# A new order for a kernel of recurrent attention and a gated layer: transfers moved between queues, transposes moved between TensorE and DMA

## The chip, the cores and the metric

The kernel runs on one core of a Trainium2 chip. The time is device time in microseconds (us) of one execution, as a median over several. Engines are named as the profile names them: PE is TensorE (PEld its weight loads), DVE is VectorE, ACT is ScalarE, POOL is GpSimd, SP is SyncE; SPq, ACTq and POOLq are the transfers that these engines issue.

## The reference, cut to what matters

```
def _attn_ref(r, k, v, w, u):                  # B, H, S, D = 4, 8, 768, 48
    state = zeros((B, H, D, D))
    for t in range(S):
        cur = einsum('bhd,bhe->bhde', u[None] * k[:, :, t], v[:, :, t])
        y[:, :, t] = einsum('bhd,bhde->bhe', r[:, :, t], state + cur)
        state = w[:, :, t, :, None] * state + einsum('bhd,bhe->bhde', k[:, :, t], v[:, :, t])

def _moe_ref(x, w_in, w_out, g_ln):            # x is y as (3072, 384); w_in 384 x 1024, w_out 1024 x 384
    h = x @ w_in
    e = exp(h - max(h));  sm = e / (sum(e) + 1e-09)
    solu = h * sm
    ln = (solu - mean(solu)) / sqrt(var(solu) + 1e-06) * g_ln
    return ln @ w_out
```

All inputs and the output are float32.

## The kernel before

The 768 steps of each of the 4 batches are cut into 6 chunks of 128 tokens. A chunk of a batch is a *unit*; the 24 units are numbered so that unit i is chunk i // 4 of batch i % 4. Within a chunk the recurrence is written as matrix products (scores between tokens, with decays folded into k and r), and a state of 384 columns goes from one chunk of a batch to the next. Each unit then goes through the second layer: hidden product, exponential, product, square, output product, scaling.

There are no loops over units in the program text. `ORDER` is a string of words written in one sequence; a word is a stage, a unit number and, after a point, how it is done. A loop at the end of the kernel calls the stage for each word:

```
    for word in ORDER.split():
        word, _, how = word.partition(".")
        name = word.rstrip("0123456789")
        stages[name](int(word[len(name):]), how)
```

Every engine goes through its own part of this sequence in order (`InOrder` ties each instruction to the one before it on the same engine); between engines only data dependences and reuse of buffers hold. Buffers are rings: 7 tiles for each loaded input, 10 for `lw` and `vb`, 6 for `kp`, `kr` and `dv`, 4 for the others. PSUM has four single slots (`s0` to `s3`) and two double ones (`b0`, `b1`), named in the word. A transfer that SP or ACT issues also waits, in the built program, for the completion of the transfer eight places before it among those of SP and ACT together, since eight semaphores are used in turn; those of POOL have eight of their own.

The words of one unit, in the order of its data:

- `LW`, `LK`, `LR`, `LV` load w, k, r and v, 192 KB each in rows of 48 floats; the letter after the point is the issuing engine (`s` SP, `a` ACT, `p` POOL). `LI0` to `LI2` load w_in (512 KB each), `LO0` and `LO1` w_out (768 KB each), `LU` and `LG` u and the gain.
- `lw` is the logarithm of w (ACT), `cum` its cumulated sums (PE, two products), `ex` the exponentials of these (ACT), `kp` the scaled k and r (DVE). `p`, `q` (POOL) and `dg` (DVE), `dv` (POOL) make the term with u. `vb` rounds v to bf16.
- `krk` and `krr` transpose the scaled k and r on PE, four products each, and `kr` copies them out of PSUM (DVE or ACT). `KD` in their place is one DMA transpose issued by SP, from `kp` straight to `kr`.
- `M` is the scores (8 products), `m` their copy to SBUF: by DVE with the mask in one instruction, or by ACT with the mask as `sel` on POOL. `S`, `et`, `st` are the state.
- `Y` is the attention output. With `n` the term `dv` is added by DVE in `y`, with `i` PE adds it with one more product and ACT copies. `X` and `xT` transpose y (PE, then a copy by DVE or ACT), or `XD` does it by DMA.
- `H` is the hidden product, `e` its exponential (ACT), `he` the product of both (DVE), `hq` the squares (ACT), `Oa` and `Ob` the output product in two halves. `sq`, `qm`, `lv` give the scale, `o` applies it (DVE or ACT), `out` stores 192 KB (by SP unless a letter says otherwise).
- For units that have the word `HD`, the hidden product is turned the other way, tokens in the rows: six products with 512 columns instead of 24 with 128, sums from ACT's accumulator instead of from products with a column of ones, and `HD` transposes `he` by DMA before `Oa`.
- `hot` makes dummy products on a tile of zeros, as many as its number says, which nobody reads. `wi`, `gw`, `mn` and `ce` prepare the weights; the last unit's layer is cut into halves (`Ha`, `Hb`, ... `Mal`, `outl`, `outr`).

The lines that the steps below touch:

```
    by_token = {int(word[2:]) for word in ORDER.split() if word[:2] == "HD"}
    def turned_kr(i, x):
        sp.dma_start_transpose(out=kr_s[i % NKP], in_=kp_t[i % NKP].rearrange("t j h d -> t (j h d)"))
    def load_v(i, x):
        queue[x].dma_start(out=v_t[i % NIO], in_=rows_of(v, i))
```

Of the kernel before, what the change touches and what calls it, by code (L numbers as in the profile page):

```python
# [26 lines left out]
dg2 krk4.s0 LK5.s m3.d krr4 vb2.a p4 H0.b0 y1.a kr4.a dg3 dv2 st0 et1 e0 LR5.s M4.b1 LV4.p S2.s3 m4.d Y2.ns0
X1.s1 et2 gw0.a LW6.s q4 lw5 he0 gw1.a LK6.s cum5.b1 vb3.p gw2.a gw3.p st1 ex5 xT1.d S3.s2 st2 H1.b0 gw5.a dv3
y2.d gw6.a dg4 LR6.s gw7.p gw4.a Y3.is1 e1 X2.s3 LW7.s kp5 mn0.s0 vb4.p y3.a he1 p5 xT2.a LK7.s lw6 X3.s1 et3
krk5.s3 hq0 dv4 ce1 cum6.b1 LR7.s H2.b0 ce5 LV5.p ex6 ce3 LW8.s ce2 xT3.a p6 krr5 ce0 e2 Y4.is1 LK8.s kp6 LV6.p  # L30
y4.a he2 lw7 LR8.s S4.s1 kr5.a q5 H3.b1 LW9.s ce7 LV7.p hq1 ce4 M5.b0 LK9.s ce6 e3 q6 X4.s3 st3 Oa0.s0 m5.d
LR9.s vb5.p hq2 krk6.s2 p7 Ob0 lw8 he3 LW10.s xT4.a krr6 q7 cum7.b0 et4 sq0 vb6.a Oa1.s3 LK10.s qm0 kr6.d ex7
LV8.p dg5 cum8.b1 hq3 S5.s2 kp7 p8 LR10.s Ob1 ex8 st4 LV9.p LW11.s H4.b0 dg6 lw9 kp8 lv0 p9 LK11.s et5 o0.a
krk7.s1 dg7 sq1 e4 M6.b1 LV10.p st5 LR11.s krr7 Oa2.s0 qm1 kr7.d vb7.a q8 LW12.s m6.a he4 S6.s2 Ob2 dv5 et6 lv1
st6 LK12.s dv6 M7.b1 o1.a cum9.b0 m7.d sq2 lw10 Y5.ns1 q9 LR12.s ex9 Oa3.s3 p10 y5.d lw11 cum10.b1 qm2 kp9
LW13.s X5.s2 lv2 Ob3 sel6 ex10 xT5.d LK13.s dg8 cum11.b0 o2.a vb8.p krk8.s1 kp10 krk9.s2 ex11 p11 krr8 out0
Y6.ns0 sq3 kr8.d krr9 hq4 H5.b1 vb9.p LR13.s kp11 dv7 kr9.a qm3 dg9 q10 LW14.s krk10.s1 e5 M8.b0 y6.d Oa4.s2 dv8
m8.d LK14.s lw12 X6.s0 LR14.s LV11.p lv3 krr10 Ob4 he5 lw13 o3.a out1.p LW15.s M9.b0 xT6.a dg10 krk11.s3 p12
m9.a cum12.b1 kr10.d LK15.s Y7.ns0 krr11 q11 ex12 y7.d S7.s1 LR15.s kr11.d H6.b0 sq4 hq5 dv9 kp12 LV12.s q12 et7
lw14 X7.s0 st7 Y8.ns3 e6 p13 qm4 M10.b1 xT7.d y8.d S8.s1 out2 m10.a he6 krk12.s0 vb10.p S9.s3 sel9 LV13.s krr12  # L40
et8 et9 cum13.b1 lv4 st8 H7.b0 ex13 dg11 dv10 LW16.s st9 kr12.a vb11.p kp13 Oa5.s1 LK16.s out3.p e7 LR16.s o4.d
S10.s0 p14 krk13.s3 lw15 he7 M11.b1 LW17.s et10 out4.p krr13 m11.a X8.s2 Ob5 sel10 kr13.d LK17.s hq6 cum14.b0
st10 vb12.p M12.b1 dg12 LR17.s ex14 S11.s3 q13 m12.d Oa6.s0 sq5 xT8.a sel11 hq7 Y9.ns2 kp14 cum15.b1 q14 Ob6
et11 ex15 qm5 y9.d KD14 st11 p15 H8.b0 lv5 kp15 lw16 LW18.s o5.a vb13.p dg13 LK18.s X9.s2 LV14.p sq6 Y10.ns3 e8
xT9.d KD15 Y11.ns1 qm6 y10.d S12.s2 dv11 lw17 he8 cum16.b1 lv6 Oa7.s3 LR18.s LV15.p o6.a y11.d et12 LV16.s ex16
M13.b0 dv12 dg14 Ob7 st12 m13.a dv13 LW19.s kp16 X10.s0 Y12.ns1 xT10.a out5.p M14.b0 lw18 H9.b1 m14.d out6.p sq7
# [5 lines left out]
H13.b1 qm10 dg17 ex19 out8.p xT14.d o9.d dv16 lv10 kp19 Y15.ns1 e13 S15.s3 vb17.p S16.s2 o10.d out9.p KD19 hq11
H14.b0 y15.d sel16 he13 lw21 LV21.s et15 et16 vb18.p Oa11.s0 LK22.s e14 st15 q18 LR22.s cum20.b1 hq12 Y16.ns1
he14 vb19.p Ob11 q19 ex20 st16 M18.b0 p20 sq11 X15.s3 y16.d m18.a S17.s2 xT15.d Oa12.s1 vb20.p kp20 et17 hq13
sel17 cum21.b0 qm11 st17 KD20 H15.b1 lv11 dg18 q20 ex21 o11.d out10 dv17 Ob12 e15 kp21 LW23.s sel18 X16.s3
LK23.s S18.s2 lw22 he15 KD21 Oa13.s0 et18 out11.p hq14 LV22.p M19.b0 dg19 M20.b1 HD15 sq12 m19.a xT16.d Ob13
qm12 m20.d p21 lv12 Y17.ns3 lw23 cum22.b0 vb21.p y17.d H16.b1 ex22 dv18 st18 dg20 o12.a dv19 kp22 Y18.ns3 sq13
e16 out12 X17.s2 sel19 Oa14.s1 LR23.s qm13 y18.d hq15 KD22 xT17.d M21.b0 q21 he16 Y19.ns3 X18.s2 Ob14 m21.a dv20
xT18.d HD16 y19.d p22 cum23.b1 sq14 lv13 dg21 H17.b0 ex23 o13.d dv21 qm14 out13 kp23 X19.s2 sel21 Y20.ns3 e17
S19.s0 xT19.d KD23 H18.b1 y20.d q22 lv14 he17 hq16 p23 XD20 Oa15.s2 o14.d et19 e18 q23 M22.b0 st19 Ob15 HD17  # L60
vb22.p m22.a Oa16.s3 he18 Y21.ns1 LV23.s hq17 sel22 M23.b0 y21.d Ob16 m23.d XD21 sq15 hq18 H19.b1 qm15 dg22 HD18
sq16 lv15 qm16 Y22.ns0 dg23 dv22 e19 Oa17.s1 o15.d vb23.p H20.b0 y22.d lv16 dv23 he19 XD22 Ob17 e20 out14 H21.b1
HD19 sq17 hq19 he20 Y23.ns2 Oa18.s0 out15 e21 o16.d HD20 H22.b0 y23.d hq20 qm17 he21 out16 Ob18 e22 HD21 X23.s3
Oa19.s2 xT23.d lv17 he22 Ha23.b1 sq18 hq21 Ob19 qm18 HD22 Hb23 sq19 ea23 qm19 o17.d Oa20.s3 lv18 out17 lv19
o18.d Oa21.s1 eb23 o19.d Ob20 out18.p hq22 hea23 out19 Ob21 sq20 hqa23 Oa22.s0 qm20 heb23 sq21 lv20 Sa23.s2 qm21
hqb23 Ob22 o20.d lv21 Sb23 out20 sq22 Mal23.s3 qm22 sq23 o21.d lv22 Mbl23 qm23 out21 Mar23.s1 o22.d lv23 Mbr23
# [558 lines left out]
```

## Time and profile before

| | us |
|---|---|
| median of 3 timed runs | 148.57 |
| lowest, highest of them | 147.11, 152.67 |
| the profiled execution | 151.26 |
| its span, first to last instruction | 149.6 |

| engine | busy us | share of the span |
|---|---|---|
| PE | 130.8 | 87% |
| DVE | 122.4 | 82% |
| ACT | 122.5 | 82% |
| POOL | 112.3 | 75% |

The page gives the busy share of each engine in 40 slices of the span, with PEclk, the clock that TensorE was granted, in tenths; then the chain of work that ended last, followed back from the end; then groups of instructions and transfers. In the chain, a piece named DMA is time in which the next instruction waited for that transfer. The matmul durations of the groups overlap, so the cost of a product on PE is read from the chain, where starts follow each other: 1.34 us for the 24 hidden products of a unit, 1.66 for its output products (1.32 where `HD` is used), 0.33 for scores, 0.33 for cum, 0.46 for state, 0.37 for Y, 0.17 for X, 0.45 for the 8 transposes of k and r. Every instruction of the stages is recorded at one helper's line (L87), so groups are told apart by their tiles.

### The profile page before, as it was taken

What the parts mean: (1) busy time and instruction counts of PE and PEld (TensorE: products, weight loads), DVE (VectorE), ACT (ScalarE), POOL (GpSimd) and SP (SyncE); (2) the same over time, 40 slices, a digit from 0 to 9 for tenths busy, and PEclk for the clock granted to TensorE, in tenths of its full rate; (3) what the DMA queues carried; (4) which work ended last, traced back from release to release, by engine and by line L of the source; (5) the groups of instructions that cost most, each with busy time, mean ns of one, the idle gap of its engine ahead of it and who ended that gap; (6) DMA issues with size and microseconds to landing.
All of it is one profiled execution on the core that took longest, in us unless ns stands there. A gap on an engine that the chain in (4) does not pass through costs nothing.

```text
span 149.6 us, 4642 instructions
## 1 busy us (share of the span) xinstructions
PE 130.8 (87%) x1801; PEld 96.4 (64%) x1808; DVE 122.4 (82%) x230; ACT 122.5 (82%) x266; POOL 112.3 (75%) x144
## 2 busy tenths in 40 slices
PE   6719776599899999999999998599999799999980
PEld 2216445397778787987879795398766566556660
DVE  7135989949999999999998999176999798968671
ACT  3535648959999999999999989349999789979891
...
PEclk9975899959999999999999999659999999999999
DMA  5999999989999989999999999999669979679744
GB/s 103 263 258 216 324 327 339 227 170 200 275 223 226 237 178 226 239 232 233 222 189 190 285 227 193 269 208 236 122 159 255 182 180 135 132 177 234 161 163 158
DMA packets 107495, 32.06 MB, mean 214 GB/s; under 512 B 103177, under 2 KB 105618, under 8 KB 107474
## 3 DMA queue, kind: packets, MB, share of 16 engines
q1 hardware_dynamic: 101856, 23.41, 79.8%
...
q10 hardware_dynamic: 3266, 0.69, 2.2%
...
## 4 chain that ended last, share of the span: by engine, by line
PE 54%; DMA 20%; ACT 13%; POOL 6%; issue 3%; DVE 1%; POOLq 0%; DVEq 0%
PE h_ps L87 18%; PE o_ps L87 17%; DMA kr<-kp 10%; ACT e L87 6%; PE s_ps L87 5%; DMA win_f<-in_moe_w_in_dram 5%; PE cum_ps L87 4%; DMA kr_in<-in_r_dram 3%; PE m_ps L87 3%; PE y_ps L87 3%; PE kr_ps L87 3%; DMA w_in<-in_w_dram 2%; POOL q L87 2%; PE x_ps L87 2%; POOL p L87 1%
## 5 line engine op out<-in xcount | busy, mean ns | idle before, releaser
L87 DVE TENSOR_TENSOR he<-h_ps,e 128x1024 bf16<-128x1024 f32 (+1 forms) x25 | 29.4, 1177 | 5.3 <-ACT e L87 5.1
L87 PE MATMUL o_ps<-w,he 128*128 128x385 bf16 (+2 forms) x144 | 32.2, 312 | 0.1
L87 ACT ACTIVATE e<-h_ps 128x1024 bf16<-128x1024 f32 (+1 forms) x25 | 24.8, 992 | 6.5 <-PE h_ps L87 6.4
L87 DVE TENSOR_TENSOR kp<-cum_ps,kr_in 128x768 bf16<-128x768 f32 x24 | 22.8, 951 | 6.5 <-DMA kr_in<-in_r_dram 5.1
L87 PE MATMUL h_ps<-xT,win_sb 128*128 128x128 bf16 x384 | 26.7, 231 | 0.0
L87 PEld LDWEIGHTS <-hq 128*128 128x128 bf16 x192 | 18.1, 98 | 12.8 <-issue 0.7
L87 POOL TENSOR_TENSOR p<-kr_in 128x384 bf16<-128x384 f32 x24 | 24.0, 1001 | 2.8 <-DMA kr_in<-in_r_dram 2.5
L87 PEld LDWEIGHTS <-win_sb 128*128 128x128 bf16 x384 | 24.6, 104 | 1.0 <-issue 0.3
L87 POOL TENSOR_TENSOR dv<-vb,dg 128x384 bf16<-128x384 bf16 x24 | 19.7, 828 | 5.2 <-DVE dg L87 2.5
L87 POOL TENSOR_TENSOR q<-p,u_bc 128x384 bf16<-128x384 bf16 x24 | 21.9, 913 | 0.5
L87 ACT ACTIVATE cum_ps<-cum_ps 128x768 f32<-128x768 f32 x24 | 19.3, 805 | 2.9 <-PE cum_ps L87 2.9
L87 PE MATMUL o_ps<-inv_col,e 128*128 128x1 bf16 x128 | 20.9, 167 | 0.0
L87 PE MATMUL o_ps<-one_col,hq 128*128 128x1 bf16 x128 | 20.4, 164 | 0.4 <-ACT o_ps L87 0.4
L87 PEld LDWEIGHTS <-kp 128*128 128x128 bf16 x192 | 12.9, 102 | 8.0 <-DVE kp L87 5.6
L87 ACT ACTIVATE hq<-he 128x1024 bf16<-128x1024 bf16 (+1 forms) x17 | 17.2, 1014 | 0.0
L87 DVE TENSOR_TENSOR m<-m_ps,uts 128x1024 bf16<-128x1024 f32 x13 | 15.8, 1218 | 1.2 <-PE m_ps L87 1.1
...
L87 PEld LDWEIGHTS <-kr 64*128 64x128 bf16 (+1 forms) x272 | 10.9, 98 | 7.5 <-DMA kr<-kp 3.4
L87 ACT ACTIVATE lw<-w_in 128x384 bf16<-128x384 f32 x24 | 12.4, 525 | 2.8 <-DMA w_in<-in_w_dram 2.6
L87 PEld LDWEIGHTS <-he 128*128 128x128 bf16 x144 | 13.4, 96 | 1.4 <-DVE o L87 0.3
L87 ACT CAST m<-m_ps 128x1024 bf16<-128x1024 f32 x11 | 11.2, 1018 | 2.8 <-PE m_ps L87 2.7
...
## 6 DMA issues: line engine op xcount, KB each, us to landing
...
```

Of the source, the lines that this page charges most:

```text
L87: made = make(*args, **kwargs)
```

## The change

Only the string `ORDER` differs; the functions are the same. Word by word, leaving the places aside:

| words | before | after |
|---|---|---|
| `LV` by POOL | 17 units: 0, 1, 4 to 11, 14, 15, 17 to 20, 22 | 13 units: 0 to 12, among them 2, 3 and 12 |
| `LI`, `LO` | `LI` and `LO1` by POOL, `LO0` by SP | all five by SP |
| `LW`, `LK`, `LR` by ACT | w of 1, k of 1, r of 0 | w of 1, 2, 8 to 11, 14; k of 2, 8, 16; r of 1, 11, 14, 15, 16 |
| `LG` | SP | ACT |
| k and r turned by DMA (`KD`) | units 14 to 23 | units 16, 17, 19, 21, 22, 23 |
| `he` turned by DMA (`HD`) | units 15 to 22 | units 12 to 22 |
| y turned by DMA (`XD`) | units 20, 21, 22 | units 21, 22 |
| `out` by POOL | 1, 3 to 9, 11, 18 | 0, 1, 2 |
| `outr` | SP | ACT |
| dummy products (`hot`) | 6, 4, 3, 2 | 7, 3, 2, 4, 2, 3 |
| `kr` copies | 9 DVE, 5 ACT | 14 DVE, 4 ACT |
| `xT` copies | 14 DVE, 7 ACT | 20 DVE, 2 ACT |
| `Y` with the extra product, `y` by ACT | 4 units: 0, 1, 3, 4 | 6 units: 0, 2, 4, 6, 8, 10 |
| `m` by ACT with `sel` | 11 units | 11 units, others |
| `vb` by ACT | 5 units | 4 units |
| `gw` by POOL | 2 of 8 | 3 of 8 |
| `o` by ACT | 8 units | 8 units, others |

The places of nearly all words move too. The diff, cut to the start, the middle and the end:

```
-pc0 LW0.s LW1.a LU0.a LK0.s hot6.s3 LG0.s LW2.s LV0.p LV1.p lw0 LR1.s lw1 LW3.s cum0.b0 ur0 LR0.a cum1.b1 LK2.s
-LK1.a us0.s0 ex0 hot4.s3 LW4.s lw2 vb0.p uc0 ex1 kp0 p0 LR2.s S0.s1 q0 cum2.b0 et0 LI0.p krk0.s2 ex2 kp1 LK3.s
-krr0 p1 LR3.s kr0.d krk1.s3 gs0.s0 LI1.p krr1 dg0 gc0 LK4.s M0.b1 kr1.a hot3.s2 dv0 m0.d LR4.s vb1.a q1 lw3 kp2
-S1.s2 lw4 M1.b1 LI2.p m1.d krk2.s0 LV2.s p2 cum3.b0 Y0.is3 ex3 krr2 dg1 LO0.s q2 y0.a kr2.d X0.s3 p3 kp3 M2.b1
...
-cum17.b1 lv7 he10 p17 S13.s2 ex17 Ob8 o7.a p18 kp17 M15.b0 sq8 et13 xT12.a S14.s3 vb15.p m15.d KD17 hq9 H11.b1
-LV17.p lw19 dg15 LK20.s dv14 qm8 Y13.ns0 st13 e11 LR20.s H12.b0 y13.d LV18.p LW21.s lv8 he11 et14 q16 Oa9.s2
-LK21.s e12 st14 dv15 cum18.b1 hq10 Y14.ns0 he12 LV19.p Ob9 LR21.s ex18 y14.d X13.s3 q17 M16.b0 LW22.s lw20 kp18
-Oa10.s0 vb16.a LV20.p sq9 m16.a dg16 M17.b1 KD18 xT13.d Ob10 p19 o8.d m17.a qm9 X14.s3 out7.p cum19.b0 sq10 lv9
...
-ol23.a out22 outl23.a or23.d outr23
+pc0 LK0.s LU0.a LW1.a LW0.s hot7.s3 LK1.s LR0.s LV0.p ur0 LW3.s lw0 LR2.s LW2.a cum0.b0 LR1.a us0.s0 hot3.s3 ex0
+LW4.s LK2.a LR3.s kp0 p0 lw1 uc0 cum1.b1 hot2.s3 q0 lw2 ex1 cum2.b0 LK3.s LV1.p dg0 lw3 krk0.s1 kp1 ex2 LV2.p
+krr0 hot4.s3 LI0.s vb0.a kr0.a p1 LG0.a M0.b1 dv0 kp2 LK4.s krk1.s2 krr1 LR4.s q1 m0.d cum3.b0 krk2.s3 LI1.s p2
+S0.s0 hot2.s1 LI2.s kr1.d vb1.a LW5.s ex3 q2 dg1 M1.b1 krr2 et0 Y0.is1 lw4 kp3 LV3.p y0.a kr2.a dg2 cum4.b0 p3
...
+M15.b0 q17 he10 LR20.s Ob8 m15.a p18 Y13.ns3 xT11.d cum17.b1 dg15 X12.s1 dv14 y13.d H11.b0 ex17 xT12.d q18 hq10
+kp17 Y14.ns0 sel15 sq8 S13.s3 e11 KD17 qm8 y14.d H12.b1 dg16 dv15 et13 lw19 he11 LW21.s p19 S14.s1 LK21.s e12
+Oa9.s0 st13 LR21.s vb16.p lv8 q19 he12 M16.b0 lw20 Ob9 out7 o8.a p20 m16.d et14 X13.s3 sq9 out8 M17.b1 xT13.a
...
+out22 outl23.a or23.d outr23.a
```

More of the change, by code (lines that the diff above doesn't have):

```diff
@@ L21 @@
 ORDER = """
-pc0 LW0.s LW1.a LU0.a LK0.s hot6.s3 LG0.s LW2.s LV0.p LV1.p lw0 LR1.s lw1 LW3.s cum0.b0 ur0 LR0.a cum1.b1 LK2.s
-LK1.a us0.s0 ex0 hot4.s3 LW4.s lw2 vb0.p uc0 ex1 kp0 p0 LR2.s S0.s1 q0 cum2.b0 et0 LI0.p krk0.s2 ex2 kp1 LK3.s
-krr0 p1 LR3.s kr0.d krk1.s3 gs0.s0 LI1.p krr1 dg0 gc0 LK4.s M0.b1 kr1.a hot3.s2 dv0 m0.d LR4.s vb1.a q1 lw3 kp2
-S1.s2 lw4 M1.b1 LI2.p m1.d krk2.s0 LV2.s p2 cum3.b0 Y0.is3 ex3 krr2 dg1 LO0.s q2 y0.a kr2.d X0.s3 p3 kp3 M2.b1
-wi1.a xT0.d krk3.s0 q3 LW5.s m2.d cum4.b0 krr3 ex4 hot2.s3 dv1 LV3.s kr3.d wi0.p Y1.is3 kp4 M3.b1 wi2.a LO1.p
@@ L27 @@
[L27 to L46, printed above, removed]
@@ L47 @@
-LK19.s hq8 q15 y12.d KD16 X11.s2 H10.b0 e9 qm7 p16 xT11.d he9 LR19.s vb14.p X12.s0 Oa8.s1 e10 sel13 LW20.s
-cum17.b1 lv7 he10 p17 S13.s2 ex17 Ob8 o7.a p18 kp17 M15.b0 sq8 et13 xT12.a S14.s3 vb15.p m15.d KD17 hq9 H11.b1
-LV17.p lw19 dg15 LK20.s dv14 qm8 Y13.ns0 st13 e11 LR20.s H12.b0 y13.d LV18.p LW21.s lv8 he11 et14 q16 Oa9.s2
-LK21.s e12 st14 dv15 cum18.b1 hq10 Y14.ns0 he12 LV19.p Ob9 LR21.s ex18 y14.d X13.s3 q17 M16.b0 LW22.s lw20 kp18
-Oa10.s0 vb16.a LV20.p sq9 m16.a dg16 M17.b1 KD18 xT13.d Ob10 p19 o8.d m17.a qm9 X14.s3 out7.p cum19.b0 sq10 lv9
@@ L52 @@
[L52 to L66, printed above, removed]
@@ L67 @@
-ol23.a out22 outl23.a or23.d outr23
+pc0 LK0.s LU0.a LW1.a LW0.s hot7.s3 LK1.s LR0.s LV0.p ur0 LW3.s lw0 LR2.s LW2.a cum0.b0 LR1.a us0.s0 hot3.s3 ex0
+LW4.s LK2.a LR3.s kp0 p0 lw1 uc0 cum1.b1 hot2.s3 q0 lw2 ex1 cum2.b0 LK3.s LV1.p dg0 lw3 krk0.s1 kp1 ex2 LV2.p
+krr0 hot4.s3 LI0.s vb0.a kr0.a p1 LG0.a M0.b1 dv0 kp2 LK4.s krk1.s2 krr1 LR4.s q1 m0.d cum3.b0 krk2.s3 LI1.s p2
+S0.s0 hot2.s1 LI2.s kr1.d vb1.a LW5.s ex3 q2 dg1 M1.b1 krr2 et0 Y0.is1 lw4 kp3 LV3.p y0.a kr2.a dg2 cum4.b0 p3
+krk3.s2 m1.d LO0.s krr3 ex4 X0.s1 LO1.s q3 st0 wi0.a LK5.s M2.b1 S1.s3 kp4 LV4.p et1 xT0.a m2.d vb2.a krk4.s0
@@ new lines @@
+wi1.p krr4 hot3.s1 kr3.d p4 LR5.s wi2.a dg3 M3.b0 dv1 Y1.ns1 st1 LW6.s kr4.a H0.b1 m3.d dv2 lw5 q4 vb3.a y1.d
+gs0.s2 M4.b0 gc0 e0 S2.s0 m4.d X1.s3 Y2.is1 gw1.p et2 gw0.a dg4 cum5.b0 gw2.a S3.s2 xT1.d dv3 y2.a he0 ex5 X2.s3
+Y3.ns1 gw3.p LK6.s gw6.a st2 H1.b1 et3 xT2.d gw7.a LR6.s y3.d gw4.p gw5.a st3 X3.s0 LW8.a xT3.d e1 vb4.p mn0.s3
+LW7.s kp5 LV5.p LK8.a he1 LK7.s lw6 S4.s1 p5 hq0 krk5.s2 cum6.b0 LR7.s ce6 dv4 krr5 H2.b1 ce3 ex6 LR8.s ce0
+LV6.p kr5.a kp6 Y4.is0 LK9.s q5 et4 LW9.a ce2 krk6.s2 H3.b0 lw7 ce1 vb5.p e2 ce5 p6 LR9.s ce7 krr6 y4.a ce4
@@ new lines @@
+LV7.p e3 X4.s0 LK10.s he2 Oa0.s3 p7 hq1 kr6.d cum7.b1 q6 Ob0 lw8 he3 LW10.a LR10.s p8 S5.s2 ex7 st4 M5.b0 xT4.d
+LV8.p m5.a Oa1.s1 kp7 LK11.s sq0 q7 et5 M6.b0 dg5 LW11.a cum8.b1 m6.d lw9 LW12.s krk7.s0 LV9.p Ob1 ex8 st5
+LR11.a krr7 sel5 H4.b0 qm0 lw10 kp8 sq1 lv0 LK12.s vb6.p kr7.d hq2 p9 krk8.s2 LR12.s cum9.b1 o0.d Y5.ns0 e4 qm1
+q8 dg6 Oa2.s3 dg7 ex9 dv5 krr8 he4 Ob2 LW13.s hq3 LV10.p y5.d cum10.b0 sq2 lv1 kp9 p10 Oa3.s0 o1.a LK13.s qm2
+ex10 kr8.d LV11.p M7.b1 Ob3 LR13.s dg8 m7.a kp10 q9 krk9.s1 lv2 X5.s2 LK14.s M8.b1 xT5.d out0.p sq3 hq4 krr9
@@ new lines @@
+o2.d S6.s2 LV13.s dv6 qm3 m8.d H5.b0 et6 LW14.a vb7.p lw11 LV12.p st6 lv3 LW15.s krk10.s3 cum11.b1 kr9.d LR14.a
+Y6.is2 sel7 ex11 dg9 krr10 o3.d Oa4.s1 y6.a LK15.s vb8.p kp11 e5 Y7.ns0 dv7 X6.s2 kr10.d lw12 M9.b1 q10 Ob4 m9.a
+y7.d LW16.s xT6.d dv8 krk11.s3 he5 LR15.a S7.s0 p11 sq4 lw13 cum12.b1 krr11 et7 LV14.s dg10 ex12 H6.b0 vb9.p
+kr11.d hq5 p12 kp12 Y8.is2 LV15.s LK16.a vb10.p st7 X7.s3 e6 q11 M10.b1 LV16.s xT7.d krk12.s0 qm4 m10.d Oa5.s3
+y8.a out1.p LR16.a S8.s2 dv9 LW17.s he6 lv4 krr12 cum13.b1 lw14 vb11.p LV17.s Ob5 lw15 sel9 kr12.d ex13 H7.b0
@@ new lines @@
+LK17.s sq5 o4.a dv10 qm5 kp13 et8 lv5 p13 Y9.ns0 st8 e7 LR17.s M11.b1 y9.d S9.s1 q12 o5.d m11.a Y10.is2 he7
+vb12.p krk13.s0 X8.s3 hq6 p14 M12.b1 LW18.s krr13 xT8.d cum14.b0 et9 LV18.s m12.a q13 st9 Oa6.s3 dg11 ex14
+vb13.p LK18.s cum15.b1 kr13.d Ob6 vb14.p ex15 kp14 q14 LR18.s S10.s1 y10.a kp15 out2.p M13.b0 et10 LW19.s hq7
+krk14.s0 X9.s2 dv11 dg12 krr14 H8.b1 sq6 st10 LK19.s lw16 p15 m13.a qm6 kr14.d out3 p16 dg13 X10.s1 S11.s0 e8
+xT9.d cum16.b0 xT10.d out4 sel11 Oa7.s2 ex16 he8 LR19.s S12.s1 et11 q15 Ob7 kp16 LW20.s et12 lv6 vb15.p o6.a
@@ new lines @@
+M14.b1 st11 dv12 LV19.s H9.b0 sq7 lw17 qm7 st12 sel12 lv7 m14.d LK20.s hq8 Y11.ns0 sel13 krk15.s3 e9 dg14
+Y12.ns1 out5 H10.b1 y11.d p17 o7.a KD16 he9 lw18 dv13 krr15 e10 X11.s0 Oa8.s2 kr15.d LV20.s q16 y12.d out6 hq9
+M15.b0 q17 he10 LR20.s Ob8 m15.a p18 Y13.ns3 xT11.d cum17.b1 dg15 X12.s1 dv14 y13.d H11.b0 ex17 xT12.d q18 hq10
+kp17 Y14.ns0 sel15 sq8 S13.s3 e11 KD17 qm8 y14.d H12.b1 dg16 dv15 et13 lw19 he11 LW21.s p19 S14.s1 LK21.s e12
+Oa9.s0 st13 LR21.s vb16.p lv8 q19 he12 M16.b0 lw20 Ob9 out7 o8.a p20 m16.d et14 X13.s3 sq9 out8 M17.b1 xT13.a
@@ new lines @@
+vb17.p Y15.ns2 m17.a LV21.s qm9 st14 cum18.b0 LW22.s S15.s3 y15.d ex18 sel17 X14.s1 dg17 Oa10.s2 LK22.s et15 lv9
+kp18 vb18.p lw21 cum19.b1 dv16 HD12 st15 H13.b0 ex19 o9.d p21 hq11 xT14.d kp19 krk18.s3 q20 Ob10 e13 dg18 KD19
+vb19.p H14.b1 sq10 hq12 dv17 he13 q21 krr18 e14 X15.s0 dg19 HD13 cum20.b0 dv18 qm10 Oa11.s1 kr18.d lv10 xT15.d
+vb20.p S16.s3 he14 ex20 LR22.s Y16.ns0 LW23.s hq13 Ob11 y16.d HD14 kp20 cum21.b1 sq11 et16 Oa12.s0 ex21 qm11
+o10.d out9 H15.b0 lv11 kp21 hq14 krk20.s2 st16 KD21 M18.b1 o11.d e15 krr20 S17.s3 kr20.d S18.s1 LK23.s m18.a
@@ new lines @@
+he15 X16.s2 out10 Ob12 LR23.s et17 lw22 sel18 M19.b1 xT16.d M20.b0 HD15 et18 sq12 st17 Oa13.s2 m20.a qm12 m19.d
+vb21.p Y17.ns3 dv19 LV22.s lv12 Ob13 hq15 dg20 sel20 cum22.b1 y17.d H16.b0 o12.d ex22 p22 st18 Y18.ns3 lw23 kp22
+X17.s0 q22 e16 Oa14.s1 xT17.d KD22 dv20 y18.d M21.b1 sq13 S19.s0 m21.a he16 X18.s3 Ob14 et19 cum23.b1 qm13 dg21
+HD16 sq14 H17.b0 ex23 qm14 xT18.d dv21 st19 lv13 kp23 p23 Y19.ns3 e17 Y20.ns0 y19.d KD23 H18.b1 vb22.p y20.d
+hq16 q23 he17 out11 X19.s3 sel21 Oa15.s0 o13.a out12 xT19.d lv14 dg22 M22.b0 HD17 e18 Y21.ns2 m22.d dv22 Oa16.s3
@@ new lines @@
+o14.a Ob15 LV23.s y21.d X20.s1 he18 XD21 sq15 hq17 M23.b0 Y22.ns2 Ob16 qm15 m23.d lv15 HD18 H19.b1 sq16 hq18
+xT20.d dg23 vb23.p Oa17.s1 y22.d e19 dv23 H20.b0 qm16 XD22 o15.a he19 lv16 Ob17 out13 e20 HD19 H21.b1 sq17 hq19
+he20 out14 Y23.ns2 Oa18.s0 e21 y23.d HD20 H22.b0 o16.d hq20 qm17 he21 X23.s2 Ob18 e22 xT23.d HD21 Oa19.s3 lv17
+he22 Ha23.b1 sq18 hq21 out15 Ob19 qm18 o17.d HD22 Hb23 ea23 Oa20.s2 sq19 lv18 qm19 hea23 out16 lv19 Oa21.s1
+o18.d hq22 out17 Ob20 o19.d out18 Ob21 out19 eb23 sq20 hqa23 Oa22.s0 qm20 heb23 lv20 Sa23.s3 sq21 hqb23 Ob22
@@ L68 @@
+qm21 o20.d lv21 Sb23 out20 sq22 Mal23.s2 qm22 sq23 o21.d lv22 Mbl23 qm23 out21 Mar23.s1 o22.d lv23 Mbr23 ol23.a
+out22 outl23.a or23.d outr23.a
 """
```

## The prediction

> **What bounds the kernel now.** I read the page's table of 40 slices first, then the chain that ended last, then the timeline around its two longest pieces, then busy time by stage.
>
> ```profile
> PE   6719776599899999999999998599999799999980
> PEclk9975899959999999999999999659999999999999
> DMA  5999999989999989999999999999669979679744
> ```
>
> A slice is 149.6 / 40 = 3.74 us. TensorE is never idle for long from slice 10 (37 us) to slice 23; before that and at slice 25 it is. Its clock is down in slices 2 to 4, 8, 25 and 26, each next to a gap. The chain gives the gaps a cause:
>
> ```profile
> 4.38 5.18 DMA kr_in<-in_r_dram
> ...
> 15.63 7.39 DMA win_f<-in_moe_w_in_dram
> ...
> 30.10 2.57 PE h_ps L87 x24
> ...
> 87.44 7.62 DMA kr<-kp
> 95.11 0.61 PE m_ps L87 x8
> ...
> 98.30 2.56 PE h_ps L87 x24
> ...
> 111.38 6.60 DMA kr<-kp
> ```
>
> Columns are start, length, what. The ramp waits for r of unit 0, then for the third part of w_in (landed at 23.02). From 38 to 87 us the chain is TensorE alone. At 87.44 the scores of unit 17 (M17) begin to wait for the turned k and r (KD17), and when they come TensorE runs at half clock: 24 hidden products take 2.56 us at 98.3 and 1.34 elsewhere.
>
> ```profile
> core 0: us, PE busy (x) PEld busy (x) DVE busy (x) ACT busy (x) POOL busy (x), PEclk, DMA share, GB/s
> 50.00:60.00 10.00, 10.00 (x168) 7.89 (x166) 9.88 (x18) 9.87 (x23) 9.98 (x14) 1.00 0.97 202
> 60.00:70.00 10.00, 10.00 (x184) 8.48 (x182) 9.79 (x18) 9.88 (x19) 9.42 (x13) 1.00 0.99 229
> 90.00:100.00 10.00, 7.84 (x92) 5.72 (x91) 6.34 (x13) 6.47 (x14) 7.04 (x11) 0.72 1.12 223
> ```
>
> In the middle all four engines are full at once, so work moved from one to another is not free there. One unit takes about 5.2 us (hidden products of units 2 and 12 start at 35.3 and 87.6: 52.3 / 10), so a microsecond won in the ramp is kept only if the middle doesn't give it back.
>
> **What the Trainium skill says.** "TensorE: Matmul & The Clock Gate", Part 1, has the clock halve after an idle window of about 3.4 us and return after about as long of sustained work. The trace agrees in kind: TensorE idles from 92.9 to 95.1, and its clock is 0.50 from 95.1 to 101.3; the gap was only 2.2 us, so a gap shorter than the window can do it. "DMA: Bandwidth & Descriptors", Issuing engines are not separate DMA queues, says that transfers of SP, ACT and GpSimd share the same 16 engines and that another issuer saves only issue time. The DMA share near 1.0 through the first 90 us fits: moving transfers between queues adds no bandwidth.
>
> **The change part by part.** The sum is made against the profiled execution, 151.26 us (span 149.6 and 1.66 around it).
>
> *Start and weights.* r of unit 0 was issued by ACT behind the logarithm, at 4.38, and landed at 9.6; it becomes SP's fourth transfer, and SP issued its fourth and fifth at 2.81 and 3.24. With the median 5.2 us to landing it is there at about 8.2: 1.5 us earlier for the first scaling (kp0, 9.69). r of unit 1 goes the other way, to ACT behind w of unit 2, about 5.0 + 5.2 = 10.2, no later than kp1 ran (10.64). The w_in parts leave GpSimd (issued 11.63, 13.20, 15.63) for SP places 10, 13 and 14, which SP reached at 10.40, 13.22 and 15.00. In front of the third part now stand all transfers of units 0 to 4, but no longer half of w_out (issued 17.37, before it landed), so it should land at 21 to 22.5 instead of 23.0. GpSimd loses three issues of 0.59 and one of 0.82 in the ramp and gains a gain step of 1.24. Six more dummy products (21 for 15) take 0.2 to 0.4 us each where TensorE idles; if they stop the half clock at 30 us, the 2.57 us piece shrinks by 1.2. I take 1.5 us off; bounds 4.2 off (3 from the loads, 1.2 from the clock) and 1 on (w_in parts in SP's order hold back k and r of unit 4).
>
> *The full middle, 38 to 90 us.* Counting moved operations of units 0 to 12 at their rows: ACT loses two kr copies (2 x 1.01), four x copies (4 x 0.49), two v casts (1.04) and a net two output scalings (1.14), and gains three y copies (3 x 0.48) and a net one score copy (1.02): 3.7 us less. DVE gains two kr copies (2 x 0.68), four x copies (4 x 0.35), two output scalings (1.22), and loses three y sums (1.65) and one score copy (1.22): 1.1 more. GpSimd: two casts (1.0) and a mask (1.09) more, one v issue (0.94) less: 1.1 more, before its output issues go. TensorE: three more 128x384 products for y (0.16 each): 0.5. Against ACT's 3.7 stand 11 transfers that ACT now issues here (w of 8 to 11 and 14, k of 8 and 16, r of 11, 14, 15 and 16). The trace has three 192 KB issues on ACT, 0.42 to 0.48 us each, the same moment's on SP 2.34:
>
> ```profile
> 5.06 2.34 SPq L87 DMA_DIRECT2D kr_in<-in_k_dram  x1
> 5.11 0.42 ACTq L87 DMA_DIRECT2D kr_in<-in_k_dram  x1
> ```
>
> So 11 x 0.42 = 4.6 us, of which some lies under a running activation (the issue at 4.38 ran beside a logarithm at 4.44). I take a loss of 0.5 us; bounds 1 gained (issues hidden) and 6.5 lost (11 x 0.93, SP's median, all bare, less 3.7).
>
> *Units 12 to 16, where the stall is.* k and r of 14, 15, 18 and 20 are turned by TensorE again: 8 transposes, 0.45 us at chain lengths, four times 1.8; four DVE copies of 0.68 (2.7). The he of 12, 13 and 14 turned by DMA shortens TensorE: hidden 1.34 to 1.30, output 1.66 to 1.32, so 3 x 0.38 = 1.1 less; ACT pays 3 x 0.59 for sums and small squares where it is a third idle (6.47 of 10). TensorE: +0.7, of which +0.9 - 1.1 by unit 15. The transfers matter more. Before, between 84.2 and 87.5 SP issued KD16, r and w of unit 19 to 20 and KD17, while GpSimd issued two v loads, then two more. Dividing the queue shares on the page by bytes (ACT's three 192-byte-row loads: 2.2% for 0.69 MB) gives an estimate of 0.94 us of all 16 engines for a load; SP's 79.8% less its 76 loads and its larger rows leaves about 27% for 21 transposes, near 2.1 us for a kr or he. KD16, KD17, two loads and four v loads are 9.8 us of transfer from 84.2 on, to 94.0 by this estimate; KD17 landed at 95.1. Afterwards, v of 14 to 20 come one by one on SP and KD14 and KD15 are gone: between the readiness of kp16 and KD17 lie some six loads and stores and KD16, about 8 us of transfer, in about 10 us of products. KD17 should then take the median 4.0 us, not 7.6.
>
> Its cover shrinks, too. From kp17 to M17 the old order has M15, S14, H11, Y13, H12, Oa9, cum18, Y14, Ob9, X13, M16 and Oa10, 7.5 us; the new one Y14, S13, H12, S14, Oa9, M16, Ob9 and X13: 0.37 + 0.46 + 1.30 + 0.46 + 0.83 + 0.33 + 0.83 + 0.17 = 4.7 us. 4.0 and a little queueing against 4.7: nearly no stall. What the stall cost: from 92.9 to 101.3 TensorE did M17, the rest of an output, x, cum, hidden and y, 3.4 us at full clock, in 8.4: 5.0 lost. I take 4.5 back; bounds 5.0 back and 2.9 lost again (a KD17 as slow as before, 9.4 from kp17: idle 4.7, half clock over the next 6.2 us costs 3.1, 7.8 in all).
>
> *Late.* KD21 took 6.6 us against 5.7 us of cover; the new order puts 7.9 us of products between KD21 and M21: 1 us back. kr18, kr20 and x of 20 on TensorE cost it 1.1. Nothing, bounds 1 either way. Seven outputs leave GpSimd for SP (0.58 each), where GpSimd is nearly idle already (1.33 of 10 after 130): worth nothing. The last half output goes out by ACT behind the other half's 0.37: 0.1 at most.
>
> Sum: -1.5 + 0.5 - 4.5 + 0 = -5.5, so 145.8. With four engines full a new order meets waits that rows can't show, and I add 0.5: 146.3. The three timed runs, 147.11 to 152.67, lie around the profiled 151.26; the stall with its half clock may be shorter in the fast ones, so the full 5.5 is not taken from their median. Against it 146.3 is 1.5% less, inside the 2% that a measurement here can tell from no change.
>
> **The rivals.**
> - *Everything lands* (chance 0.15). w_in 3 us earlier, no half clock at 30 us, no stall: -4.2 + 0.5 - 5.0 = -8.7, 142.6. For it: all three are waits for transfers in the chain. Against it: DMA share is 0.97 to 1.07 in the first 30 us, so the same bytes come at the same rate.
> - *The stall only moves* (0.15). The half clock at 95 us is this one execution's, and late transposes of he 12 to 14 fill the queues the old ones left: ramp gain and 0.7 of new products cancel, 148.5.
> - *ACT's queue holds the middle* (0.30), slower. ACT works in order and is 98.8% busy from 50 to 70; every transfer it issues first waits, in the program, for the one eight places earlier among SP's and ACT's, and SP in turn for ACT's. Behind it stand cum's exponentials and e, for which DVE's kp and he and then TensorE wait. If each of 11 holds it 0.93 us, the middle loses 6.5 instead of 0.5, and loads run less far ahead, so the queue is full again at KD17: no more than 3 of the 4.5 return. 151.26 - 1.5 + 6.5 - 3 = 153.3. It decides from about 0.45 us bare per issue on (3.7 freed plus 1.2 of idle, over 11). For it: SP's issues are long in this stretch. Against it: ACT's own were 0.42 beside SP's 2.34, and those eight places earlier should long have landed.
>
> **How the numbers follow.** Forecast 146.3 with chance 0.40, own range 144.5 to 148.5 (a third of it under 145.6, the 2% bound). Rivals 142.6, 148.5 and 153.3. Range 142.6 to 153.0: half of the slow rival's chance and a little of the fast one's lie outside. Faster 0.29: the fast rival's 0.15 and 0.14 of the forecast. Slower 0.30: the slow rival. Same 0.41.
>
> **What would show it.** Right: win_f's last part lands before 22.5 and the first hidden products start by 22.8; no m_ps wait of over 1 us for kr<-kp near unit 17, PEclk at 9 through slices 24 to 28; ACT issues near 0.42. Wrong: ACT idle with cum_ps or e late between 40 and 85 and TensorE under 10.0 there; a kr<-kp piece of over 7 us in the chain again; or the hidden products of unit 2 no earlier than 35.3.

## The result and the profile after

The change makes the kernel slower: a median of 155.47 us (153.84 to 157.32) against 148.15 us (147.11 to 152.67), a ratio of 1.048 (after over before) with a 95% interval of 1.033 to 1.063. The forecast was 146.3 with a range that ended at 153.0. The profiled execution took 157.32 us with a span of 155.4, to be set against 151.26 and 149.6; both were among the longer executions of their kernels, which a ratio leaves out and a median does not, so pieces of the two traces are compared with each other only, and small differences of time are read from the ratio.

First the table of 40 slices of the kernel after, a slice now 3.89 us, and for comparison ACT's row of the kernel before:

```profile
PE   6697676797849999949499999999999999999980
ACT  3385967977361998572987899899999988999880
PEclk9999999999965999999959999999999999999997
DMA  5999999999899999999998063399999999789943
```

```profile
ACT  3535648959999999999999989349999789979891
```

The gap that the kernel before had in slices 24 to 26 is gone: from slice 20 (78 us) TensorE is full almost to the end, in slice 20 itself at half clock. In its place stand holes at slices 11, 17 and 19, counted from 0 (from 42.7, 66.0 and 73.8 us), in the stretch that was full before. ACT has four of its own there, and deeper ones: 3, 1, 5 and 2 at slices 10, 12, 16 and 18. Three of them lie one slice ahead of a hole of TensorE's; at the fourth, slice 12, TensorE is busy at half clock. Busy time by stage of the kernel after, in the columns of the prediction, and then the first of these stages in the kernel before:

```profile
40.00:50.00 10.00, 7.42 (x84) 5.58 (x83) 6.35 (x10) 3.34 (x7) 9.69 (x12) 0.71 1.05 225
60.00:70.00 10.00, 8.03 (x145) 6.67 (x142) 7.91 (x16) 6.78 (x12) 9.98 (x14) 1.00 0.99 203
70.00:80.00 10.00, 7.96 (x132) 6.33 (x130) 7.34 (x14) 7.06 (x17) 4.02 (x6) 0.91 1.08 233
90.00:100.00 10.00, 9.95 (x180) 8.44 (x179) 9.85 (x17) 9.13 (x15) 8.73 (x11) 1.00 0.46 101
```

```profile
40.00:50.00 10.00, 10.00 (x159) 7.61 (x157) 10.00 (x18) 9.97 (x22) 9.75 (x12) 1.00 1.08 240
```

From 40 to 50 us ACT works for 3.34 of 10 us where it had 9.97, and TensorE for 7.42 at a mean clock of 0.71 where it was full. From 90 to 100, where TensorE lost most before (7.84 at 0.72), it is now at 9.95 and 1.00. The starts of the product `he` (DVE), read from the timelines, cut the span into pieces:

| us | before | after | difference |
|---|---|---|---|
| start to he of unit 3 | 42.20 | 39.67 | -2.5 |
| he of unit 3 to he of unit 8 | 33.75 | 47.37 | +13.6 |
| he of unit 8 to he of unit 22 | 61.15 | 54.89 | -6.3 |
| he of unit 22 to the end | 12.5 | 13.5 | +1.0 |
| span | 149.6 | 155.4 | +5.8 |

So the ramp won more than the 1.5 that was forecast, the later part more than the 4.5, and one piece in the middle lost more than both. Where it was lost is seen in ACT's own timeline (start, length, operation, and in brackets the idle time ahead of it with what ended it; an issue, ACTq, does not count as work, so a bracket takes in the issue just before it):

```profile
42.59 0.44 ACTq L88 DMA_DIRECT2D w_in<-in_w_dram  x1
43.14 0.80 ACT L88 ACTIVATE cum_ps<-cum_ps 128x768 f32<-128x768 f32 x1 [2.86 <-DMA kr_in<-in_k_dram]
...
49.86 0.37 ACTq L88 DMA_DIRECT2D kr_in<-in_r_dram  x1
50.28 0.52 ACT L88 ACTIVATE lw<-w_in 128x384 bf16<-128x384 f32 x1 [3.17 <-DMA w_in<-in_w_dram]
...
66.49 0.41 ACTq L88 DMA_DIRECT2D kr_in<-in_r_dram  x1
66.94 0.17 ACT L88 ACTIVATE sq<-o_ps 128x2 f32<-128x2 f32 x1 [2.67 <-PE h_ps L88]
...
72.95 0.37 ACTq L88 DMA_DIRECT2D kr_in<-in_r_dram  x1
73.42 0.29 ACT L88 ACTIVATE lv<-sq,qm 128x1 f32<-128x1 f32 x1 [2.88 <-DVE kr L88]
```

Four times ACT is idle for about 3 us (2.86 + 3.17 + 2.67 + 2.88 = 11.6 in all, of which the four issues are 1.6), and each time the first thing that it does next is the issue of a load: LW10, LR11, LR15, LR16. The issue itself is short, 0.37 to 0.44 us, just as it was priced; the rest lies in front of it, 2.2 to 2.8 us each time. The releaser in the bracket belongs to the activation behind the issue, and for the last two it names an engine that had long been done. The chain of the kernel after names what two of the issues waited for:

```profile
17.26 8.86 DMA wout_f<-in_moe_w_out_dram
...
36.19 6.38 DMA kr_in<-in_k_dram
42.59 0.44 ACTq L88
...
48.63 2.52 PE h_ps L88 x24
...
67.20 5.72 DMA kr_in<-in_r_dram
72.95 2.70 DMA kr_in<-in_r_dram
```

k of unit 9, issued by SP at 36.19, lands at 36.19 + 6.38 = 42.57, and ACT's issue of w of unit 10 starts at 42.59. ACT needs nothing from k of unit 9: in the built program LW10 waits for that transfer, whose semaphore it is to use next. In the same way a load of r, that of unit 17, ends at 67.20 + 5.72 = 72.92, and LR16, which waits for it in the built program, is issued at 72.95. For the other two the built program names w of unit 12 (LR11) and v of unit 15 (LR15); in the trace these land at 49.78 and 66.41, and the issues start at 49.86 and 66.49. The piece at 48.63 is the half clock after the first hole: 24 hidden products in 2.52 us.

### The profile page after: what moved, and what is told of

It is laid out like the page before. It is cut to its first block, busy times and chain, and to the rows that moved or that the text cites. A ratio compares the mean times of both kernels' runs of the same rounds, so it can differ in the third digit from the quotient of the medians.

```text
span 155.4 us, 4549 instructions
## 1 busy us (share of the span) xinstructions
PE 133.9 (86%) x1741; PEld 94.1 (61%) x1749; DVE 125.5 (81%) x239; ACT 120.4 (77%) x269; POOL 103.6 (67%) x131
## 4 chain that ended last, share of the span: by engine, by line
PE 52%; DMA 18%; SPq 9%; ACT 9%; POOL 4%; DVE 2%; issue 2%; ACTq 0%; DVEq 0%
PE o_ps L88 17%; PE h_ps L88 16%; SPq L88 9%; DMA wout_f<-in_moe_w_out_dram 6%; DMA kr_in<-in_r_dram 5%; DMA kr_in<-in_k_dram 4%; PE y_ps L88 4%; PE m_ps L88 4%; PE s_ps L88 4%; PE cum_ps L88 4%; PE kr_ps L88 3%; ACT e L88 3%; DMA w_in<-in_w_dram 3%; PE x_ps L88 2%; ACT cum_ps L88 1%
## 5 line engine op out<-in xcount | busy, mean ns | idle before, releaser
L88 PE MATMUL o_ps<-w,he 128*128 128x385 bf16 (+2 forms) x120 | 27.2, 315 | 0.2
L88 PEld LDWEIGHTS <-hq 128*128 128x128 bf16 x192 | 18.0, 99 | 12.5 <-issue 1.6
L88 PE MATMUL h_ps<-xT,win_sb 128*128 128x128 bf16 x312 | 21.1, 226 | 0.1
L88 PEld LDWEIGHTS <-win_sb 128*128 128x128 bf16 x312 | 19.2, 102 | 0.7 <-ACT win_sb L88 0.3
L88 POOL TENSOR_SCALAR_AFFINE_SELECT m<-m 128x1024 bf16<-128x1024 bf16 x11 | 12.0, 1090 | 8.9 <-ACT et L88 6.0
L88 PE MATMUL o_ps<-w,hq 128*128 128x385 bf16 x88 | 17.3, 328 | 0.1
L88 PE MATMUL o_ps<-inv_col,e 128*128 128x1 bf16 x104 | 17.1, 168 | 0.0
L88 PE MATMUL m_ps<-kr 64*128 64x128 bf16 x192 | 9.8, 225 | 8.4 <-DVE kp L88 3.9
L88 PE MATMUL o_ps<-one_col,hq 128*128 128x1 bf16 x104 | 16.5, 164 | 0.1
L88 PE MATMUL h_ps<-win_sb,xT 128*128 128x512 bf16 x60 | 15.7, 378 | 0.3
L88 PE MATMUL kr_ps<-ident,kp 128*128 128x128 bf16 x144 | 14.0, 227 | 1.1 <-DVE kp L88 1.1
```

Source lines behind the costliest of these rows:

```text
L88: made = make(*args, **kwargs)
```

## The experiments

Each time below is compared with runs of the kernel before on the same chip at that time, whose medians lay between 148.94 and 149.61 us. The kernel after was not run again beside them, so its 155.47 us and 1.048 are those given above. Theory A is that ACT stands still at its added loads. Theory B blames the weights, which all went to SP.

**ACT's eleven loads back to SP, in the order after.**

```diff
-LW8.a LW9.a LW10.a LW11.a LW14.a LK8.a LK16.a LR11.a LR14.a LR15.a LR16.a
+LW8.s LW9.s LW10.s LW11.s LW14.s LK8.s LK16.s LR11.s LR14.s LR15.s LR16.s
```

> The changed kernel with the 11 loads that ACT issues from unit 8 on (w of 8 to 11 and 14, k of 8 and 16, r of 11, 14, 15, 16) given back to SP at the same places of the order. Theory A (ACT, in order, stands still in front of such a load until an earlier transfer has landed; four such gaps of 2.9, 3.2, 2.7 and 2.9 us, 11.6 in all, in the trace): the gaps vanish, 145 to 148 us against the changed kernel's 155.5, since the ramp's gain and the end of the stall at unit 17 stay. Theory B (the weights and v that moved to SP's queue make loads late, and ACT would wait for w anyway): SP now has 11 more, so 155 or more. Theory C (the new order itself, DVE with 4.4 us more work): within 2 us of 155.5.

Measured: 150.26 us, ratio 1.007 (1.004 to 1.011) where the whole change has 1.048. With no load on ACT the stops in front of its loads are gone, and TensorE has full clock until the last slice:

```profile
PEclk9999999999999999999999999999999999999996
40.00:50.00 10.00, 8.18 (x131) 6.30 (x128) 7.93 (x15) 6.66 (x15) 9.95 (x13) 1.00 1.04 224
```

So 5 to 6 us, most of the loss, hang on the issuing engine of eleven loads alone. The 145 to 148 us that theory A expected are missed, however, and the time does not fall below before: ACT now waits five times for w between 20 and 50 us, the longest being

```profile
46.95 0.52 ACT L86 ACTIVATE lw<-w_in 128x384 bf16<-128x384 f32 x1 [2.44 <-DMA w_in<-in_w_dram]
```

**The same eleven loads alone, in the kernel before.**

```diff
-LW8.s LW9.s LW10.s LW11.s LW14.s LK8.s LK16.s LR11.s LR14.s LR15.s LR16.s
+LW8.a LW9.a LW10.a LW11.a LW14.a LK8.a LK16.a LR11.a LR14.a LR15.a LR16.a
```

> The kernel before with the same 11 loads moved from SP to ACT and nothing else. Theory A: 5 to 10 us slower, 153 to 158, with gaps on ACT in front of its loads. Theory B: 148 to 150, because SP's queue has fewer transfers and the weights come by GpSimd. Theory C: 148 to 149, 11 issues of 0.4 us partly hidden.

Measured: a median of 155.72 us; four runs from 151.45 to 157.15 gave no interval. Three of them lie above 155 us, where only one of the 23 runs of before does; the fourth is 1.8 above the 149.61 of before. So the loads alone cost time, but how much is known only roughly, 2 to 6 us; the spans of the two traces differ by 4.0 (153.6 against 149.6). ACT's timeline shows one long stop, again in front of the issue of a load:

```profile
41.87 0.43 ACTq L86 DMA_DIRECT2D w_in<-in_w_dram  x1
42.34 1.06 ACT L86 ACTIVATE hq<-he 128x1024 bf16<-128x1024 bf16 x1 [5.29 <-DMA kr_in<-in_r_dram]
```

The load is w of unit 9. In the built program it waits for r of unit 9, which lands at 41.84. No other of the eleven has a stop here. The he of unit 3 moves from 42.20 to 44.34 and that of unit 4 from 48.79 to 53.52.

**Only the four loads with a stop in front, back to SP.**

```diff
-LW10.a LR11.a LR15.a LR16.a
+LW10.s LR11.s LR15.s LR16.s
```

> The changed kernel with only four of ACT's loads back on SP: w of 10 and r of 11, 15 and 16, those in front of which ACT stood still for 2.9, 3.2, 2.7 and 2.9 us. Theory A (the wait for an earlier transfer's landing, not the issue of 0.4 us, is the price): nearly all of the 5 us returns, 150 to 152. Rival A' (each load on ACT costs, whichever it is): four of 11, so 153.5 to 154. Rival A'' (another load on ACT becomes the one that waits, since the places of the waits shift): 153 to 156.

Measured: 151.15 us, ratio 1.018 (1.006 to 1.030). Four of eleven bring back the larger part of what all eleven do, about 3 of the 4.1%. The other seven keep their issue lengths of 0.37 to 0.46 us; the stops that are left stand at four of them and are shorter, 1.04 to 2.38 us with the issue:

```profile
43.32 0.52 ACT L86 ACTIVATE lw<-w_in 128x384 bf16<-128x384 f32 x1 [2.17 <-DMA kr_in<-in_k_dram]
...
54.33 0.52 ACT L86 ACTIVATE lw<-w_in 128x384 bf16<-128x384 f32 x1 [1.04 <-DMA kr_in<-in_k_dram]
...
56.47 0.80 ACT L86 ACTIVATE cum_ps<-cum_ps 128x768 f32<-128x768 f32 x1 [1.20 <-POOL dv L86]
...
64.89 1.02 ACT L86 ACTIVATE e<-h_ps 128x1024 bf16<-128x1024 f32 x1 [2.38 <-POOL m L86]
```

In the kernel after none of these four (LW11, LW14, LR14, LK16) had a stop of over 0.6 us, so rival A'' is right in part: other loads became the ones that wait. The price of a load on ACT is not a fixed sum per issue. In these traces it is next to nothing where the earlier transfer has landed, and a stop of 1 to 5 us where it has not. No run gave four of the other seven back to SP, which would have tested rival A' directly.

**The weights back to GpSimd, ACT's loads kept.**

```diff
-LI0.s LI1.s LI2.s LO1.s
+LI0.p LI1.p LI2.p LO1.p
```

> The changed kernel with the three parts of w_in and the second half of w_out issued by GpSimd again, ACT's loads as changed. Theory A: ACT still stands in front of its loads, but what it waits for was issued late partly because large transfers held SP's semaphores between 17 and 36 us; a part comes back, 150 to 154. Theory B: most comes back, 147 to 150. Theory C: 154 to 157.

Measured: 157.51 us, ratio 1.055 (1.047 to 1.064), no better than the change, where theory A too had expected a part back. The ramp of this trace loses 5.6 us (he of unit 3 at 45.25 for 39.67), and ACT's stops only come at other instructions:

```profile
ACT lv L86 <- DMA kr_in<-in_r_dram: 4.2, 1, 4.2
ACT e L86 <- DMA kr_in<-in_k_dram: 3.6, 1, 3.6
ACT lw L86 <- DMA kr_in<-in_r_dram: 1.9, 1, 1.9
ACT sq L86 <- DMA v_in<-in_v_dram: 1.7, 1, 1.7
```

(total us, times, longest). A scale `lv` that "waits for r" stands behind a load of ACT's that waits, and so do the other three. Theory B falls as the cause of the main loss.

**v of units 14 to 22 back to GpSimd.**

```diff
-LV14.s LV15.s LV17.s LV18.s LV19.s LV20.s LV22.s
+LV14.p LV15.p LV17.p LV18.p LV19.p LV20.p LV22.p
```

> The changed kernel with v of 14, 15, 17, 18, 19, 20 and 22 issued by GpSimd again, ACT's loads as changed. Theory A: the third and fourth gap (at 64 and 71 us, where SP issues v of 14, 15 and 16 in 1.3 us each in front of what ACT waits for) shrink: 151 to 154. Theory B: 148 to 151. Theory C: 155 to 157, GpSimd having 6.5 us more to do.

Measured: 155.73 us (153.33 to 157.98): no change of the time that these four runs tell, and theory A's 151 to 154 is missed. The stops did move. That in front of LR15, which waited for v of unit 15, is gone, that in front of LR16 is 1.96 us for 2.88, and that in front of LR11 is 4.75 for 3.17. So v on SP has a part in where ACT stops, and giving it back to GpSimd does not remove the loss.

**What is left: w_out.** Two kernels take ACT's loads back to SP and move w_out as well, once to GpSimd, once its second half three places later on SP.

```diff
-LO0.s LO1.s
+LO0.p LO1.p
```

> The changed kernel with ACT's 11 later loads on SP, and both halves of w_out issued by GpSimd at their places. In the run with ACT's loads on SP alone, SP needed 9.4 us for the three transfers behind w_out (19.0 to 28.5), and ACT then waited 5.7 us for w between 23 and 47 us, none of which the kernel before has. Theory A2 (those waits are what is left): they shrink to under 2 us, 145 to 147.5, faster than the kernel before. Theory C (what is left is the new order and DVE's extra work): no change, 149.5 to 151. Theory D (the bytes, not the queue: the DMA share is 1.0 either way): 149 to 151, the waits for w move to other loads.

Measured: 150.57 us, ratio 1.007 (0.995 to 1.019), as with w_out on SP. In its profiled execution the waits for w in the middle shrink (he of unit 3 to 4 takes 7.85 us for 10.16 with w_out on SP), and the ramp loses more than that:

```profile
16.90 11.22 DMA w_in<-in_w_dram
```

This piece of its chain is a load of w that takes 11.22 us beside w_out; he of unit 3 starts at 44.46 instead of 39.68. That w_out does this is not shown. A further kernel, given below, differs from this one only in v from unit 14 on; there the same load, issued at 16.94, takes 8.7 us, he of unit 3 starts at 40.88, and he of unit 3 to 4 takes 9.78 us. So most of the shift is a difference between two executions.

```diff
-X0.s1 LO1.s q3 st0 wi0.a LK5.s ... LR5.s ... LW6.s
+X0.s1 q3 st0 wi0.a LK5.s ... LR5.s ... LW6.s LO1.s
```

> The order after with its eleven ACT loads back on SP, and the second half of w_out (LO1, 768 KB) moved three places back in SP's order, behind k and r of unit 5 and w of unit 6. Theory P (what is left of the loss is the place of w_out in SP's order): the issues of k5, r5 and w6 no longer take 4.2, 2.1 and 3.1 us, ACT's wait for w between 20 and 62 us falls from 5.7 to under 3 us without a new wait for w_out of over 1 us, and the time is 148.0 to 149.3, below the 149.6 of the kernel before. Theory D (the same bytes go out at a full DMA share up to 90 us, so a transfer moved back delays another one): the waits only change their names, and the time is that of the eleven-load kernel, 149.6 to 151.0.

Measured: 150.99 us, ratio 1.021 (1.014 to 1.027). Moving it later wins nothing, and most of the waits changed their names, as theory D has it: those of ACT for w in the middle are largely replaced by

```profile
ACT w L86 <- DMA wout_f<-in_moe_w_out_dram: 3.5, 2, 3.3
```

and he of unit 8 starts at 78.33, against 78.05 with w_out in its old place.

The further kernel had w_out and v by GpSimd together:

> As the run before it in this call, and v of 14, 15, 17 to 20 and 22 by GpSimd too. Theory A2: within 1 us of it, since after 60 us SP's queue holds nobody any more. Theory B (v on SP's queue makes loads late): 1 to 3 us faster than it.

Measured: 151.71 us, ratio 1.023 (1.013 to 1.033): v by GpSimd does not make that order faster. Whether it makes it slower stays open, since the intervals overlap.

**The weights by SP alone, in the kernel before.**

```diff
-LI0.p LI1.p LI2.p LO1.p
+LI0.s LI1.s LI2.s LO1.s
```

> The kernel before with w_in and the second half of w_out (LI0, LI1, LI2, LO1) issued by SP at the places where GpSimd issued them; LO0 is on SP already. It asks what the part of the loss is that remains when ACT's loads are gone. Theory W (the weights in SP's order hold back the loads behind them): w and k of units 5 to 9 come late, ACT waits 3 us or more for w between 20 and 60 us, the product he of unit 8 starts at 78 us or later instead of 75.95, and the time is 2 to 4 us above before. Theory O (the rest of the new order is the cause): he of unit 8 within 1 us of 75.95, the time within 1 us of before.

Measured: 151.09 us against 149.03, ratio 1.008 (1.003 to 1.013). On the question the trace is for theory O: he of unit 8 starts at 74.83, earlier than the 75.95 of before, so in this execution weights on SP don't hold back units 5 to 8. A loss of 1 to 2 us remains that the trace doesn't place: its profiled execution, 149.81, is among the shorter ones of this kernel.

**The stall at unit 17 alone.** In the kernel before, KD17 is replaced by eight transposes on TensorE and a copy:

```diff
-KD17 ... y13.d
+y13.d krk17.s0 krr17 kr17.d
```

> The kernel before with k and r of unit 17 turned by TensorE (8 transposes, 0.45 us, and one DVE copy of 0.68) instead of by DMA. It prices the stall at 93 us. If the 5.0 us that the profiled execution lost there (2.2 idle, the rest at half clock) belong to every execution: 144.5 to 146.5 against 149. If the half clock belongs to some executions alone: 147 to 148.5. If the stall only moves to unit 18 or 19: 148.5 to 150.

Measured: 146.31 us, ratio 0.989 (0.981 to 0.998). TensorE has no half clock after the ramp; he of unit 12 to 13 takes 7.55 us for 11.78. A second, longer comparison of the same kernel:

> The kernel before with k and r of unit 17 turned by TensorE instead of by DMA, once more and on its own. Theory S (the stall at unit 17 costs an ordinary execution of the kernel before 1 to 2 us): a ratio of 0.985 to 0.992, its interval below 1, about 147. Theory T (the stall was this large in the profiled execution only, as the version with units 17 and 21 suggests): 0.994 to 1.002.

Measured: 148.58 us, ratio 0.993 (0.989 to 0.997), the same 7.55 us in its trace. So the 4.2 us that the traces show at unit 17 are worth 1 to 1.6 us by the ratios. Part of them only moves forward: he of unit 8 to 12 takes 15.84 and 17.67 us in these two traces for 14.25 before, and in both TensorE stands still for 1.08 us just ahead of he of unit 12, in the first trace so:

```profile
91.20 0.32 PE L86 MATMUL cum_ps<-lw,uti_neg 128*128 128x384 bf16 x1 [1.08 <-DVE he L86]
```

This version is faster than both kernels, by less than the 2% that counts here as a difference. Unit 21 treated likewise (`KD21` out, `krk21.s3 krr21 kr21.d` behind `xT16.d`) adds nothing that the runs tell:

> The kernel before with k and r of unit 17 and of unit 21 turned by TensorE (eight transposes and a DVE copy each) instead of by DMA. With unit 17 alone the time was 146.3 and TensorE still waited 1.46 us for the turned k and r of unit 21. Theory S (each stall behind a DMA transpose is worth its idle time less the transposes that replace it): 1.46 less 0.45 on TensorE, so 1 us less again: 145.0 to 145.8. Theory T (the next late thing, he or the next transpose, takes its place): 146.0 to 147.0, and the idle stretch shows up within 10 us behind it.

Measured: 148.51 us, ratio 0.996 (0.992 to 1.001). In its profiled execution, at 152.1 us the longest of its 22, TensorE waits for an earlier transpose instead, first in the chain and then in TensorE's timeline:

```profile
99.92 6.16 DMA kr<-kp
```

```profile
106.12 0.40 PE L86 MATMUL m_ps<-kr 64*128 64x128 bf16 x8 [2.17 <-DMA kr<-kp]
```

## Why the prediction was wrong, step by step

*Start and weights, 1.5 taken off.* Right in kind, low in size: kp0 runs at 7.61 instead of 9.69, the half clock near 30 us is gone, and he of units 0 to 3 comes 1.4, 2.8, 0.1 and 2.5 us earlier, inside the bounds of 4.2 off and 1 on. Other traces agree: he of unit 3 starts at 38.29 to 39.68 in four kernels with the new ramp (after, and three of those above) and at 40.91 to 42.93 in four with the old.

*The full middle, 0.5 lost.* This is the step that failed. Between he of units 3 and 8 the trace lost 13.6 us. The step was a difference, 4.6 us for eleven issues on ACT less the 3.7 us of work that ACT gives up, and both terms were mis-sized. With ACT's loads on SP the piece takes 38.36 us: so in these traces the eleven loads cost 9.0 us (47.37 - 38.36), and the rest of the order costs 4.6 (38.36 - 33.75) where the freed work was to give 3.7 back. In the measured times the loads cost 5 to 6 us (155.47 against 150.26; 1.048 against 1.007), which is not far above 4.6. There the larger part of the miss is that the gains set beside them did not come: without the loads on ACT the kernel is still 0.7% slower than before, where by the sum it should have been much faster.

The first term took the length of an ACT issue, 0.42 us, for its price, eleven times. The length was right (0.37 to 0.48 after), but the wait is not part of it. "Perfetto Trace Analysis", DMA Instruction — HWDGE (DVE, Sync), in the Trainium skill says so: the reported window of such an issue begins when all its semaphores are satisfied. The trace agrees: LW10 has 0.44 us of issue with 2.3 of standstill ahead (the activation before it ends at 40.27). The failed sentence is the one "against" the slow rival, that "those eight places earlier should long have landed". They had not, for two reasons. The semaphores follow the order of the built program, in which the transfer ahead of LW10 with the same semaphore is k of unit 9, only four transfers of SP and ACT earlier in `ORDER`. And SP was late there. After the two parts of w_out its issues are long, in the timeline of SP's queue:

```profile
18.93 2.84 SPq L88 DMA_DIRECT2D kr_in<-in_k_dram  x1
21.81 2.83 SPq L88 DMA_DIRECT2D kr_in<-in_r_dram  x1
24.68 3.20 SPq L88 DMA_DIRECT2D w_in<-in_w_dram  x1
...
36.19 2.06 SPq L88 DMA_DIRECT2D kr_in<-in_k_dram  x1
```

The upper bound of that step, 6.5 lost, priced each of the eleven at SP's median issue, 0.93 us, so 10.2 in all. That is near the 9.0 of the traces for the wrong reason: a few stops of about 3 us with what they cost TensorE, not eleven small sums. The half clock was in no term of it: the mean clock of 0.71 over 40 to 50 us is a loss of up to 2.9 us more.

The range of the whole still missed, although the later part gave back more than the slow rival allowed, because of the second term. The 3.7 us of work taken from ACT brought nothing that can be seen: with the loads on SP it is w that ACT waits for in this stretch. What makes the rest of the order slower there stays open. Neither run that moves w_out brings he of unit 8 forward in this order (by GpSimd 80.40, later on SP 78.33, for 78.05), and the weights on SP do not delay it in the old order (74.83). The weights by GpSimd together with ACT's loads on SP were not run, nor any of the many moves of words.

*The stall at unit 17, 4.5 back.* Right for the trace. There is no wait of the scores for turned k and r in TensorE's list of the kernel after, and he of unit 12 to 13 takes 7.57 us for 11.78, 4.2 less. KD17 took 3.2 us to landing (98.22 to 101.40) where 4.0 was set. It met emptier queues than foreseen, as the loads ran ahead while the engines stood: the DMA share from 90 to 100 us is 0.46 where it was 1.12. That is no condition of the gain, however. With ACT's loads on SP and shares of 0.93 and 1.17 (w_out later) KD17 took 4.1 and 4.3 us and the piece 8.49 and 7.58. In the measured times the stall was worth 1 to 1.6 us in the old order, far less than the 4.5, as the prediction suspected of the timed runs.

*Late, nothing.* One microsecond lost behind he of unit 22, at the edge of the bounds given.

*The sum.* The pieces of the two traces add up, 151.26 - 2.5 + 13.6 - 6.3 + 1.0 = 157.1 against 157.32 profiled, and the one far from its term is the middle. Of the rivals, "ACT's queue holds the middle" named the wait and the place, though it priced the issues and not the wait; its 153.3 was 2.2 us short of the median, and its price for the middle less than half of what the trace shows. The forecast took the other side because a short issue was read as a cheap one. The signs listed as right all came true (w_in's last part landed by 21.1, first hidden products at 21.9, no wait at unit 17 and a full clock there, ACT issues near 0.42), and the first of those listed as wrong did too: ACT idle with `cum_ps` late between 40 and 50, and TensorE at 7.42 of 10.
